# Sorted block attention and a gated feed-forward block on one core: half of batch 0's q goes as fp32 through SP's queue, turns use the full array height, later heads' matrices are built later

## The chip, the core and the metric

The kernel runs on one core of one Trainium2 chip. The metric is the device time of one execution in microseconds (us). A core has TensorE (PE, matrix products, with its weight loads shown apart as PEld), VectorE (DVE), ScalarE (ACT), GpSimd (POOL) and SyncE (SP). All of them work at the same time, each through its own instructions in order, and wait for each other by semaphores. DMA transfers are issued here by POOL and by SP; each of the two has a queue of its own, and 16 DMA engines serve both. Inputs lie in HBM, working tiles in SBUF, and PE writes its results to the eight banks of PSUM, from which ACT or VectorE evict them.

## The reference

Batch 4, 8 heads, 768 positions, head width 64; 8 blocks of 96 positions. A small matrix per head is normalised five times over rows and columns (Sinkhorn). It then mixes the blocks of k and v, each block of q attends to its mixed block of k and v, and the result goes through a gated feed-forward block.

```python
P = sort_net                                   # (4, 8, 8, 8)
for _ in range(5):
    P = P - np.max(P, axis=-1, keepdims=True)
    P = np.exp(P)
    P = P / (np.sum(P, axis=-1, keepdims=True) + 1e-09)
    P = P / (np.sum(P, axis=-2, keepdims=True) + 1e-09)
k_sorted = np.einsum('bhij,bhjcd->bhicd', P, k_b)      # v_sorted likewise
scores = scale * np.matmul(q_b, k_sb.transpose(0, 1, 2, 4, 3))
scores = scores - np.max(scores, axis=-1, keepdims=True)
attn = np.exp(scores)
attn = attn / (np.sum(attn, axis=-1, keepdims=True) + 1e-09)
x = np.matmul(attn, v_sb)                      # heads side by side: (3072, 512)
g = x @ w_gate                                 # (3072, 1536)
out = (g * (1.0 / (1.0 + np.exp(-g))) * (x @ w_val)) @ w_out
```

## The kernel before

**Tiling.** The 3072 rows are cut into eight units `u` of 384 rows, two halves (four blocks of 96) of each batch. For each unit the attention of four pairs of heads `hp` is computed, its result is laid into a transposed tile `xt`, and the feed-forward block runs over 12 chunks `m` of its 1536 columns: `g` and `u` are the two up projections (L520), `th`, `gs`, `us`, `h` and `hp` the gate around them, `dn` and `oc` the down projection and the output (L548, L554). Everything is computed in bf16 with sums in fp32; the Sinkhorn steps are in fp32.

**Order.** The program is a flat list of steps. After the loads and the five Sinkhorn iterations, which are ordinary Python code, the string `ORDER` names every step with its arguments, the engine of its eviction (`a` for ACT, `d` for VectorE) and its PSUM banks (`p0` to `p7`). Each step issues its instructions on each engine's queue at that place, so the string fixes the order of work on every engine, and of the loads that POOL issues (`ldk`, `ldv`, `ldq`, `ldwg`, `ldwv`, `ldwo`).

**Loads.** All large inputs are fp32 in HBM and become bf16 on the way into SBUF; POOL issues these transfers. The order on POOL's queue is: q of batch 0, first half (`load_q0(0)`, L199), k and v of batch 0 (L189, L193), then the identity matrix is made, then the first third of the two up weights (L208), then q's second half. In the Sinkhorn loop's first iteration POOL makes some constants (`selk`, `selm`, `rmb`); behind them it issues v, weights and k of batch 1. SP issues only the small `p_sb` load at the start, and much later the outputs and a round trip of v through HBM. POOL waits before an issue until the transfer that POOL issued eight before it has landed (seen in the profile's waits).

**Start.** The Sinkhorn loop (L330 to L367) alternates one exponential on ACT (L331) with six small operations on VectorE (L332 to L337). Meanwhile PE runs filler products (`busy`, L245, whose results nobody reads) and turns q's first half: `q0_piece(half, n, eng, b)` (L249) turns four heads, one 64-wide head at a time into the upper or lower half of the partitions (L257, 12 products for one piece), and evicts the bank into `q0t`. Piece 0 is issued in iteration 3, piece 1 in iteration 4; behind piece 1 PE has fillers and four products that read `q0t` (L346). After the loop `make_zk` spreads the normalised matrices over partitions (L376 on PE, L380 and L381 on VectorE), and `make_bdk` makes the matrix `bdk` (L384) that mixes the blocks of one batch: batch 0's at once on VectorE, the others in the step `late` (L390), whose three `make_bdk` run on POOL.

**First unit.** `kp,0,n,eng,bank` mixes and turns the piece `n` of six of batch 0's k (L283, evicted into `kt` at L238 by ACT or L240 by VectorE); `v0f,n` does the same with v, and `v0t` turns it back (L302). `tqk` makes the scores of a pair of heads (L404) and needs all six pieces of `kt`; `tmax` takes their maxima on VectorE (L420), `tmt` turns these on PE (L424), `tst` makes the scores again with the maxima subtracted (L433), `texp` is the exponential on ACT (L440), `tav` the product with v (L447), `tdiv` the division on VectorE (L453, L455), `txt` the turn into `xt` (L460). `q0p,1,n` is `q0_piece` for the second half of batch 0's q. Later batches mix v with L309 (`vp`), and the units from 2 on use `qk`, `rmax`, `shift`, `expo`, `rsum`, `norm`, `turn` and `av`.

Of the kernel before, what the change touches and what calls it, by code (L numbers as in the profile page):

```python
# [9 lines left out]
FP32 = mybir.dt.float32  # L10
BF16 = mybir.dt.bfloat16
# [4 lines left out]


ORDER = """
ldwv,2 ldwg,2 late,p0 kp,0,5,a,p1 ldwo,2 kp,0,3,d,p2 kp,0,4,a,p3 ldq,1 kp,0,2,d,p4 kp,0,0,d,p5 v0f,3,a,p6
v0f,2,a,p7 v0f,5,a,p0 kp,0,1,d,p1 tqk,0,1,p2,p3 tmax,0,1 tqk,0,2,p4,p5 tqk,0,3,p6,p7 tmax,0,3 busy,3,p0 tmt,0,1,a  # L20
busy,1,p0 tst,0,1 tmax,0,2 tmt,0,3,a tqk,0,0,p0,p1 texp,0,1 busy,1,p2 tmt,0,2,a tmax,0,0 tst,0,3 texp,0,3 tst,0,2
tmt,0,0,a v0f,1,d,p2 v0f,0,a,p3 tst,0,0 texp,0,0 ldv,2 texp,0,2 ldwo,0 v0f,4,d,p6 busy,3,p2 v0t,0,0,d,p7
v0t,1,0,d,p2 v0t,0,1,a,p3 tav,0,0,p0,p1 tdiv,0,0 v0t,1,1,a,p6 tav,0,1,p4,p5 tdiv,0,1 busy,2,p2 txt,0,0,d,p7
tav,0,2,p2,p3 tdiv,0,2 tav,0,3,p0,p1 txt,0,1,d,p6 q0p,1,0,a,p4 q0p,1,1,a,p5 txt,0,2,a,p7 g,0,2,p2,0,2 g,0,1,p3,0,2
# [85 lines left out]
def kernel(  # L110
# [16 lines left out]
    nc = tc.nc  # L127

    B, H, S, D = q.shape
# [6 lines left out]
    UT = HB * BLK  # L136
# [8 lines left out]
    C0 = UT // 128  # L145

    const = ctx.enter_context(tc.tile_pool(name="const", bufs=1))
    natp = ctx.enter_context(tc.tile_pool(name="natp", bufs=1))
# [5 lines left out]
    hpool = ctx.enter_context(tc.tile_pool(name="hpool", bufs=2))  # L154
# [10 lines left out]
    def ps(name, shape, dt=FP32, parts=128):  # L165
        n = 1
        for x in shape:
            n *= x
        t = banks[:, int(name[1:]), :]
        t = (t if dt is FP32 else t.bitcast(BF16))[0:parts, 0:n]  # L170
        if len(shape) == 1:
            return t
        if len(shape) == 2:
            return t.rearrange("p (a b) -> p a b", a=shape[0])
        return t.rearrange("p (a b c) -> p a b c", a=shape[0], b=shape[1])
# [6 lines left out]
    kn, qn, vn = {}, {}, {}  # L182
# [4 lines left out]
    def load_k(b):  # L187
        kn[b] = natp.tile([128, CK, D], BF16, name="kn", tag="kv", bufs=4)
        nc.gpsimd.dma_start(out=kn[b], in_=k[b].rearrange("h (j ch c) d -> (h j ch) c d", j=NB, ch=CH))  # L189

    def load_v(b):
        vn[b] = natp.tile([128, CK, D], BF16, name="vn", tag="kv", bufs=4)
        nc.gpsimd.dma_start(out=vn[b], in_=v[b].rearrange("h (j ch c) d -> (h j ch) c d", j=NB, ch=CH))  # L193

    def load_q0(half):
        if half == 0:
            qh = natp.tile([128, 2, H, C0, D], BF16, name="qh", tag="qn", bufs=2)
            qn[0, 0], qn[0, 1] = qh[:, 0], qh[:, 1]
        nc.gpsimd.dma_start(out=qn[0, half],  # L199
                            in_=q[0][:, ds(half * UT, UT), :].rearrange("h (p c) d -> p h c d", c=C0))  # L200

    def load_q(b):
        qn[b] = natp.tile([128, H, S // 128, D], BF16, name="qn", tag="qn", bufs=2)
# [2 lines left out]
    def load_w(dst, w, n):  # L206
        f = ds(n * (DF // 3), DF // 3)
        nc.gpsimd.dma_start(out=dst[:, :, f], in_=w.rearrange("(hp p) f -> p hp f", p=128)[:, :, f])  # L208

    def load_ws(n):  # L210
        load_w(wg_sb, moe_w_gate, n)
        load_w(wv_sb, moe_w_val, n)
# [5 lines left out]
    p_sb = const.tile([BH, NB + 1, NB], FP32, name="p_sb")  # L218
    nc.sync.dma_start(out=p_sb[:, 0:NB, :], in_=sort_net.rearrange("b h i j -> (b h) i j"))
    load_q0(0)  # L220
    load_k(0)
    load_v(0)
    ident = const.tile([128, 128], BF16, name="ident")
    make_identity(nc, ident)
    load_ws(0)
    load_q0(1)

    fill = const.tile([128, 512], BF16, name="fill")
# [7 lines left out]
    def evict(eng, dst, src):  # L236
        if eng == "a":
            nc.scalar.copy(dst, src)  # L238
        else:
            nc.vector.tensor_copy(dst, src)  # L240

    def busy(n, b, cols=512):

        for _ in range(n):
            nc.tensor.matmul(ps(b, [cols]), lhsT=fill[:, 0:128], rhs=fill[:, 0:cols], start=True, stop=True)  # L245
# [3 lines left out]
    def q0_piece(half, n, eng, b):  # L249
        if ("q", half) not in tr:  # L250
            q0t = trp.tile([128, 2, HP, HB, BLK], BF16, name="q0t", tag="qt")
            tr["q", 0], tr["q", 1] = q0t[:, 0], q0t[:, 1]
        p = ps(b, [6, 128], BF16)
        for l in range(6):
            hp, c = 2 * n + l // C0, l % C0
            for x in range(2):
                nc.tensor.transpose(p[ds(64 * x, 64), l, :], qn[0, half][:, 2 * hp + x, c, :], ident)  # L257
        dst = tr["q", half][:, ts(n, 2)].rearrange("p hp i (cq c) -> p hp (i cq) c", c=C0)
        evict(eng, dst, p.rearrange("p (hp c) n -> p hp n c", c=C0))

# [69 lines left out]
    for it in range(N_ITER):  # L330
        nc.scalar.activation(P, P, AF.Exp)  # L331
        nc.vector.reduce_sum(rowred[:, :, 0], P, axis=AX.X)  # L332
        nc.vector.reciprocal(rowred, rowred)
        nc.vector.tensor_mul(P, P, rowred.to_broadcast([BH, NB, NB]))
        nc.vector.reduce_sum(colred[:, 0, :], p_sb.transpose([0, 2, 1]), axis=AX.X)
        nc.vector.reciprocal(colred, colred)
        nc.vector.tensor_mul(pbf if it == N_ITER - 1 else P, P,  # L337
                             colred.to_broadcast([BH, NB, NB]))
        if it == N_ITER - 2:
            q0_piece(0, 0, "a", "p0")  # L340
        if it == N_ITER - 1:
            q0_piece(0, 1, "a", "p1")
            busy(8, "p7", 112)
            busy(10, "p7")
            for _ in range(4):
                nc.tensor.matmul(ps("p7", [UT]), lhsT=fill[:, 0:128], rhs=tr["q", 0][:, HP - 1].rearrange("p i c -> p (i c)"),  # L346
                                 start=True, stop=True)
        if it == 0:
            selk = const.tile([BH, BH, 16], BF16, name="selk")
            nc.gpsimd.tensor_copy(selk, ident[0:BH, 0:BH].unsqueeze(2).to_broadcast([BH, BH, 16]))  # L350
            nc.gpsimd.memset(v0[:, :, :, :, D:D + 1], 1.0)

            sel = const.tile([128, HB], BF16, name="sel")
            nc.gpsimd.tensor_tensor(sel, ident[:, 0:HB], ident[:, 64:64 + HB], op=ALU.add)
            selm = const.tile([128, HB, BLK], BF16, name="selm")
            nc.gpsimd.tensor_scalar(selm, sel.unsqueeze(2).to_broadcast([128, HB, BLK]), -1.0, None, op0=ALU.mult)

            rmb = [const.tile([BLK, 2, 64], BF16, name=f"rmb{n}") for n in range(HP)]
            for t in rmb:
                nc.gpsimd.memset(t, 0.0)  # L360
        if it == 1:
            mjk = const.tile([128, 1, NB], FP32, name="mjk")
            nc.vector.reduce_sum(mjk[:, 0, :], ident.rearrange("p (h j ch) -> p j h ch", j=NB, ch=CH),
                                 axis=AX.XY)
        if it == 2:
            m1 = const.tile([128, 8, CH], FP32, name="m1")
            nc.vector.reduce_sum(m1, ident.rearrange("p (h j ch) -> p h ch j", j=NB, ch=CH), axis=AX.X)  # L367
# [4 lines left out]
    def make_zk(b0, b1, b):  # L372
        n = (b1 - b0) * NB
        p = ps(b, [n, NB])
        for b in range(b0, b1):
            nc.tensor.matmul(p[:, ts(b - b0, NB)].rearrange("p i j -> p (i j)"),  # L376
                             lhsT=selk[:, ds(b * H, H), :].rearrange("p h r -> p (h r)"),
                             rhs=pbf.rearrange("p i j -> p (i j)"), start=True, stop=True)
        zk = const.tile([128, n, NB], FP32, name=f"zk{b0}")
        nc.vector.tensor_tensor(zk, p, mjk.to_broadcast([128, n, NB]), op=ALU.mult)  # L380
        nc.vector.reduce_sum(zkr[:, b0:b1, :].rearrange("p b i -> p (b i)"), zk, axis=AX.X)  # L381

    def make_bdk(b, eng):
        eng.tensor_tensor(  # L384
            bdk[:, b],
            m1.unsqueeze(2).to_broadcast([128, H, NB, CH]),
            zkr[:, b, :].unsqueeze(1).unsqueeze(3).to_broadcast([128, H, NB, CH]),
            op=ALU.mult)

    def late(b):  # L390
        make_zk(1, B, b)
        for n in range(1, B):
            make_bdk(n, nc.gpsimd)

# [159 lines left out]
    def ffn_last(u, t, n, eng, b):  # L556
# [19 lines left out]
        busy=busy, late=late, ldk=load_k, ldv=load_v, ldq=load_q, ldwo=load_wo,  # L576
        ldwg=lambda n: load_w(wg_sb, moe_w_gate, n), ldwv=lambda n: load_w(wv_sb, moe_w_val, n),
        q0p=q0_piece, v0f=v0_piece, v0t=v0_turn, kp=k_piece, vp=v_piece, qp=q_piece, vtrip=v_turn,
        tqk=t_qk, tmax=t_max, tmt=t_maxt, tst=t_st, texp=t_exp, tav=t_av, tdiv=t_div, txt=t_xt,
        qk=qk, rmax=rowmax, shift=shift, expo=expo, rsum=rowsum, norm=norm, turn=turn, av=av,  # L580
        g=lambda *a: ffn_up(wg_sb, "g", *a), u=lambda *a: ffn_up(wv_sb, "u", *a), th=ffn_th, us=ffn_us, gs=ffn_gs,
        h=lambda u, m: ffn_h(u, m, False), hp=lambda u, m: ffn_h(u, m, True), dn=ffn_down, oc=ffn_out, dl=ffn_last)
# [33 lines left out]
```

## Time and profile before

| what | us |
|---|---|
| median of 3 runs (265.08 to 265.35) | 265.09 |
| the profiled execution: its time | 265.16 |
| the profiled execution: its span on the core | 263.1 |
| first scores (L404) start | 17.14 |
| first feed-forward product (L520) starts | 30.16 |
| PE busy with L520, weights wg and wv | 79.8 and 79.6 |
| PE busy with L548 | 70.5 |

The span runs from the core's first to its last instruction; the time of a run has some 2 us more around it. The busy time of PE counts the length of every product, and neighbours overlap, so a busy share of 97% says that PE almost always had something in work.

The transfers of the first 40 us, each with the moment of its issue on POOL, the time from issue to landing, and the first instruction that reads it:

| transfer | issued | to landing | first read |
|---|---|---|---|
| q of batch 0, half 0 | 1.24 | 5.6 | 6.84 (L257) |
| k of batch 0 | 2.31 | 8.1 | 13.00 (L283) |
| v of batch 0 | 2.86 | 12.2 | 15.08 (L283) |
| first third of w_gate | 3.95 | 13.7 | 30.16 (L520) |
| first third of w_val | 4.71 | 15.5 | 32.39 (L520) |
| q of batch 0, half 1 | 5.45 | 16.7 | 29.19 (L257) |
| v of batch 1 | 9.13 | 16.7 | 31.84 (L309) |
| k of batch 1 | 11.26 | 23.3 | 38.42 (L283) |

In the profile, PE, PEld, DVE, ACT and POOL are the engines, L283 is line 283 of the kernel, and `out<-in` names the tiles that an instruction writes and reads. A bracket at a row's end gives the idle time of the engine ahead of the instruction and what ended it. `x48` counts instructions merged into one row.

### The profile page before, as it was taken

The page shows a single profiled execution, that of the slowest core. Times are in us where ns is not written, and L with a number is a line of the kernel's source. Part 1 is how long each engine was busy: PE and PEld are TensorE (multiplying, and loading weights), DVE is VectorE, ACT ScalarE, POOL GpSimd, SP SyncE. Part 2 cuts the span into 40 slices and gives each one's busy share as a digit, 9 for nine tenths or more (in the row PEclk, how much of TensorE's full clock was granted, in tenths as well). Part 3 has the DMA queues.
Part 4 walks back from the last instruction along what each step waited for, and adds up shares of the span by engine and source line. Part 5 has one row for each costly group of instructions (what it writes and reads, how often), then busy time and mean ns, then how long its engine had stood idle before and what let it go on. Part 6 is the DMA issues. An engine that isn't in the chain of part 4 may idle for free.

```text
span 263.1 us, 6835 instructions
## 1 busy us (share of the span) xinstructions
PE 254.7 (97%) x2766; PEld 157.1 (60%) x2766; DVE 190.3 (72%) x345; ACT 154.2 (59%) x299; POOL 116.8 (44%) x152
## 2 busy tenths in 40 slices
PE   7878999999999999999999999999999999999995
PEld 7456766665566555665566555665566555655553
DVE  5775877689688896779798776977897778632460
ACT  3246787755467467866476767586566665544422
POOL 8732342433856437135632475226544672431220
PEclk9999999999999999999999999999999999999999
DMA  6999999999980902100294005920110021002103
GB/s 82 215 199 209 216 203 211 204 238 248 157 195 0 161 2 82 44 0 2 120 118 123 2 0 199 118 49 1 52 70 0 2 80 42 0 1 83 40 0 120
DMA packets 33695, 25.60 MB, mean 97 GB/s; under 512 B 21376, under 2 KB 29312, under 8 KB 33664
## 3 DMA queue, kind: packets, MB, share of 16 engines
q0 software_dynamic: 11104, 14.16, 31.4%
q1 hardware_dynamic: 22560, 11.02, 18.2%
q8 instruction: 21, 0.34, 0.5%
q14 instruction: 10, 0.08, 0.1%
HBM read 30.68 MB, written 8.65 MB: 149 GB/s over the span
## 4 chain that ended last, share of the span: by engine, by line
PE 88%; DMA 5%; DVE 3%; issue 1%; ACT 1%; POOL 1%; DVEq 0%; POOLq 0%
PE ps_ps L520 47%; PE ps_ps L548 23%; DMA vn<-in_v_dram 5%; PE ps_ps L497 3%; PE ps_ps L404 3%; PE ps_ps L283 3%; PE ps_ps L508 2%; PE ps_ps L309 2%; PE ps_ps L433 1%; PE ps_ps L270 1%; PE ps_ps L560 1%; DVE qt L240 1%; DVE xn L455 1%; PE ps_ps L447 1%; DVE v L240 0%
## 5 line engine op out<-in xcount | busy, mean ns | idle before, releaser
L539 POOL TENSOR_TENSOR h<-u_sb,gs 128x384 bf16<-128x384 f32 x65 | 58.6, 911 | 64.9 <-DVE gs L533 36.3
L520 PE MATMUL ps_ps<-xt,wg_sb 128*128 128x384 bf16 x384 | 79.8, 327 | 0.0
L520 PE MATMUL ps_ps<-xt,wv_sb 128*128 128x384 bf16 x384 | 79.6, 326 | 0.0
L533 DVE SCALAR_TENSOR_TENSOR gs<-th,ps_ps 128x384 bf16<-128x384 bf16 x96 | 51.4, 543 | 32.4 <-ACT th L525 32.0
L548 PE MATMUL ps_ps<-wo_sb,h 128*128 128x512 bf16 x276 | 70.5, 380 | 0.0
L525 ACT ACTIVATE th<-ps_ps 128x384 bf16<-128x384 f32 x96 | 46.9, 490 | 34.2 <-PE ps_ps L520 32.1
L490 POOL TENSOR_TENSOR en<-e,rs 96x384 bf16<-96x384 f32 x48 | 38.5, 822 | 55.6 <-DVE rs L485 31.1
L520 PEld LDWEIGHTS <-wv_sb 128*128 128x128 bf16 x384 | 37.2, 98 | 24.8
L520 PEld LDWEIGHTS <-wg_sb 128*128 128x128 bf16 x384 | 35.5, 98 | 25.9
L548 PEld LDWEIGHTS <-h 128*128 128x128 bf16 x276 | 26.3, 98 | 25.3 <-issue 0.2
L529 ACT ACTIVATE u_sb<-ps_ps 128x384 f32<-128x384 f32 x65 | 31.8, 490 | 10.9 <-PE ps_ps L520 7.6
L480 ACT ACTIVATE e<-e 96x768 f32<-96x768 f32 x24 | 20.2, 841 | 23.8 <-DVE e L477 23.8
L484 DVE TENSOR_REDUCE rs<-e 96x8 f32<-96x768 f32 x24 | 22.6, 941 | 10.3 <-ACT e L480 10.3
L473 DVE TENSOR_REDUCE rm<-ps_ps 96x8 f32<-96x768 f32 x24 | 22.8, 949 | 4.8 <-PE ps_ps L404 4.3
L477 DVE TENSOR_TENSOR e<-ps_ps,rm 96x768 f32<-96x768 f32 x24 | 22.9, 953 | 0.8
L541 DVE SCALAR_TENSOR_TENSOR h<-ps_ps,gs 128x384 bf16<-128x384 f32 x31 | 17.2, 557 | 2.7
L238 ACT COPY o_sb<-ps_ps 128x512 f32<-128x512 f32 x16 | 9.2, 580 | 8.6 <-PE ps_ps L548 8.6
L497 PEld LDWEIGHTS <-en 96*96 96x96 bf16 x192 | 12.0, 125 | 3.2
L245 PE MATMUL ps_ps<-fill 128*128 128x112 bf16 (+1 forms) x96 | 11.7, 290 | 2.2 <-DVE p_sb L322 1.5
L497 PE MATMUL ps_ps<-ident,en 96*96 96x96 bf16 x192 | 12.5, 209 | 0.0
L238 ACT COPY et<-ps_ps 96x768 bf16<-96x768 bf16 x13 | 10.3, 791 | 3.2 <-PE ps_ps L497 3.1
L238 ACT CAST kt<-ps_ps 128x512 bf16<-128x512 f32 x14 | 7.8, 593 | 3.8 <-PE ps_ps L283 3.7
(97 smaller groups left out, 240.6 us busy)
## 6 DMA issues: line engine op xcount, KB each, us to landing
out_dram<-o_sb SPq DMA_DIRECT2D x23, 256.0 KB, 2.0
kn<-in_k_dram POOLq DMA_DIRECT2D x4, 768.0 KB, 18.6
vn<-in_v_dram POOLq DMA_DIRECT2D x4, 768.0 KB, 14.4
qn<-in_q_dram POOLq DMA_DIRECT2D x3, 768.0 KB, 23.6
vscr<-vm SPq DMA_DIRECT2D x3, 768.0 KB, 3.3
vt<-vscr SPq DMA_DIRECT2D x3, 768.0 KB, 7.9
wg_sb<-in_moe_w_gate_dram POOLq DMA_DIRECT2D x3, 512.0 KB, 18.7
wv_sb<-in_moe_w_val_dram POOLq DMA_DIRECT2D x3, 512.0 KB, 20.4
```

Of the source, the lines that this page charges most:

```text
L238: nc.scalar.copy(dst, src)
L473: nc.vector.reduce_max(m[:, :, :, 0], st["s", u, hp], axis=AX.X)
L477: nc.vector.tensor_tensor(e, st["s", u, hp], st["m", u, hp].to_broadcast([BLK, 2, HB, BLK]), op=ALU.subtract)
L484: nc.vector.reduce_sum(rs[:, :, :, 0], st["e", u, hp], axis=AX.X)
L490: nc.gpsimd.tensor_tensor(en[:, x], st["e", u, hp][:, x], st["rs", u, hp][:, x].to_broadcast([BLK, HB, BLK]), op=ALU.mult)
L497: nc.tensor.transpose(p[:, x * HB + i, :], st["en", u, hp][:, x, i, :], ident[0:BLK, 0:BLK])
L520: nc.tensor.matmul(st[kind, u, m], lhsT=w[:, kc, ts(m, 128)], rhs=xt[u][:, kc, :], start=(kc == 0), stop=(kc == HP - 1))
L525: nc.scalar.activation(st["th", u, m], st["g", u, m], AF.Tanh, scale=0.5)
L529: nc.scalar.activation(st["us", u, m], st["u", u, m], AF.Copy, scale=0.5)
L533: nc.vector.scalar_tensor_tensor(gs, st["th", u, m], 1.0, st["g", u, m], op0=ALU.add, op1=ALU.mult)
L539: nc.gpsimd.tensor_tensor(h_t[u][:, m, :], st["us", u, m], st["gs", u, m], op=ALU.mult)
L548: nc.tensor.matmul(st["o", u, t], lhsT=h_t[u][:, m, ts(t, 128)], rhs=wo_sb[:, m, :], start=(m == 0), stop=(m == NFC - 1))
```

## The change

Four things change.

1. The first half of batch 0's q goes as fp32 into a tile of the pool of `h`, by two transfers of four heads each that SP issues right after `p_sb`. A new step `cast_q0` casts it to bf16 and lays the heads side by side: four heads on ACT after Sinkhorn iteration 1, the other four on POOL after iteration 2. The second half still comes by POOL's queue as bf16, now into a tile of that same pool, and POOL lays its heads side by side by two `cast_q0` in `late`.
2. With two heads side by side, `q0_piece` turns both by one product of the full width: 6 products for a piece instead of 12.
3. POOL makes the identity matrix before it issues the loads of k and v. The fillers around the two pieces of q are distributed anew.
4. In `ORDER`, `late` (with `make_zk` for batches 1 to 3, their `make_bdk`, and the two casts) moves from near the front, where it stood behind two weight loads, to the place after the last maximum of the first unit, behind the issue of two more loads. The last piece of k (`kp,0,1`) moves from behind the three first pieces of v to before them; the banks shift accordingly, and one filler ahead of `tmt,0,2` becomes two.

```diff
-ldwv,2 ldwg,2 late,p0 kp,0,5,a,p1 ldwo,2 kp,0,3,d,p2 kp,0,4,a,p3 ldq,1 kp,0,2,d,p4 kp,0,0,d,p5 v0f,3,a,p6
-v0f,2,a,p7 v0f,5,a,p0 kp,0,1,d,p1 tqk,0,1,p2,p3 tmax,0,1 tqk,0,2,p4,p5 tqk,0,3,p6,p7 tmax,0,3 busy,3,p0 tmt,0,1,a
-busy,1,p0 tst,0,1 tmax,0,2 tmt,0,3,a tqk,0,0,p0,p1 texp,0,1 busy,1,p2 tmt,0,2,a tmax,0,0 tst,0,3 texp,0,3 tst,0,2
+ldwv,2 ldwg,2 kp,0,5,a,p1 ldwo,2 kp,0,3,d,p2 kp,0,4,a,p3 ldq,1 kp,0,2,d,p4 kp,0,0,d,p5 kp,0,1,d,p6 v0f,3,a,p7
+v0f,2,a,p0 v0f,5,a,p1 tqk,0,1,p2,p3 tmax,0,1 tqk,0,2,p4,p5 tqk,0,3,p6,p7 tmax,0,3 busy,3,p0 tmt,0,1,a
+busy,1,p0 tst,0,1 tmax,0,2 tmt,0,3,a tqk,0,0,p0,p1 texp,0,1 busy,2,p2 tmt,0,2,a tmax,0,0 late,p2 tst,0,3 texp,0,3 tst,0,2
...
     def load_q0(half):
+        src = q[0][:, ds(half * UT, UT), :].rearrange("h (p c) d -> p h c d", c=C0)
+
         if half == 0:
-            qh = natp.tile([128, 2, H, C0, D], BF16, name="qh", tag="qn", bufs=2)
+            qh = natp.tile([128, 2, C0, H, D], BF16, name="qh", tag="qn", bufs=2)
             qn[0, 0], qn[0, 1] = qh[:, 0], qh[:, 1]
-        nc.gpsimd.dma_start(out=qn[0, half],
-                            in_=q[0][:, ds(half * UT, UT), :].rearrange("h (p c) d -> p h c d", c=C0))
+
+            qn["f", 0] = hpool.tile([128, H, C0, D], FP32, name="qf", tag="h")
+            for n in range(2):
+                h = ds(n * (H // 2), H // 2)
+                nc.sync.dma_start(out=qn["f", 0][:, h], in_=src[:, h])
+        else:
+            qn["f", 1] = hpool.tile([128, H, C0, D], BF16, name="qg", tag="h")
+            nc.gpsimd.dma_start(out=qn["f", 1], in_=src)
+
+    def cast_q0(half, n, act):
+        h = ds(n * (H // 2), H // 2)
+        (nc.scalar.copy if act else nc.gpsimd.tensor_copy)(qn[0, half][:, :, h, :].transpose([0, 2, 1, 3]),
+                                                           qn["f", half][:, h])
...
     load_q0(0)
+    ident = const.tile([128, 128], BF16, name="ident")
+    make_identity(nc, ident)
     load_k(0)
     load_v(0)
-    ident = const.tile([128, 128], BF16, name="ident")
-    make_identity(nc, ident)
     load_ws(0)
     load_q0(1)
...
             hp, c = 2 * n + l // C0, l % C0
-            for x in range(2):
-                nc.tensor.transpose(p[ds(64 * x, 64), l, :], qn[0, half][:, 2 * hp + x, c, :], ident)
+            nc.tensor.transpose(p[:, l, :], qn[0, half][:, c, ds(2 * hp, 2), :].rearrange("p x d -> p (x d)"), ident)
...
+        if it == 1:
+            cast_q0(0, 0, True)
+        if it == 2:
+            cast_q0(0, 1, False)
         if it == N_ITER - 2:
             q0_piece(0, 0, "a", "p0")
+            busy(20, "p7", 112)
+            busy(4, "p7")
         if it == N_ITER - 1:
             q0_piece(0, 1, "a", "p1")
-            busy(8, "p7", 112)
-            busy(10, "p7")
+            busy(5, "p7")
...
         for n in range(1, B):
             make_bdk(n, nc.gpsimd)
+        for n in range(2):
+            cast_q0(1, n, False)
```

## The prediction

> **What bounds the kernel now.** I read the page first: busy times, then the chain that ended last.
>
> ```profile
> span 263.1 us, 6835 instructions
> PE 254.7 (97%) x2766; PEld 157.1 (60%) x2766; DVE 190.3 (72%) x345; ACT 154.2 (59%) x299; POOL 116.8 (44%) x152
> PE 88%; DMA 5%; DVE 3%; issue 1%; ACT 1%; POOL 1%; DVEq 0%; POOLq 0%
> ```
>
> PE makes 88% of the chain. The timeline of PE shows it without a gap from 31 us to the end (one of 0.29 us at 59.4), so nearly whatever the first 31 us give or lose reaches the end one to one. The one DMA of the chain is v of batch 0. Then the chain in order of time, cut to the first scores (start, length, what):
>
> ```profile
> 2.86 12.18 DMA vn<-in_v_dram
> 15.04 0.04 issue
> 15.08 0.97 PE ps_ps L283 x48
> 16.05 1.09 ACT vT L238 x2
> 17.14 0.01 issue
> 17.14 0.74 PE ps_ps L404 x24
> ```
>
> v lands at 15.04, PE mixes three pieces of it, and the first scores (L404) begin at 17.14. The view names ACT's vT as the last step, but the scores read kt. So I looked at VectorE (start, length, engine, line, operation):
>
> ```profile
> 12.46 0.29 DVE L384 TENSOR_TENSOR bdk<-m,zkr 128x128 bf16<-128x128 f32 x1
> 13.11 0.36 DVE L380 TENSOR_TENSOR zk<-ps_ps,mjk 128x192 f32<-128x192 f32 x1 [0.36 <-PE ps_ps L376]
> 13.50 0.35 DVE L381 TENSOR_REDUCE zkr<-zk 128x24 f32<-128x192 f32 x1
> 13.77 1.88 DVE L240 CAST kt<-ps_ps 128x512 bf16<-128x512 f32 x3
> 16.40 0.69 DVE L240 CAST kt<-ps_ps 128x512 bf16<-128x512 f32 x1 [0.76 <-PE ps_ps L283]
> 17.66 0.95 DVE L420 TENSOR_REDUCE rmb<-ps_ps 96x8 bf16<-96x768 f32 x1 [0.57 <-PE ps_ps L404]
> ```
>
> The last kt piece ends at 17.09, and the scores follow 0.05 later. It is late because its matmuls (piece 1) stand behind the three v pieces on PE, hence behind v's landing.
>
> **Part 1: piece 1 of k ahead of v, and zk of the later heads out of the way.** PE's rows at this place:
>
> ```profile
> 12.81 0.26 PE L376 MATMUL ps_ps<-pbf,selk 32*128 32x64 bf16 x3
> 13.00 1.46 PE L283 MATMUL ps_ps<-bdk,kn 128*64 128x64 bf16 x80
> 15.08 0.95 PE L283 MATMUL ps_ps<-bdk,vn 128*64 128x64 bf16 x48 [0.63 <-DMA vn<-in_v_dram]
> ```
>
> Without L376 x3 the k pieces start at 12.81 instead of 13.00, one each 0.29 (1.46 for five), six end at 14.55. VectorE's first kt needs the second piece: before 13.00 + 2x0.29 + 0.19 (from matmuls to eviction, as ACT's first kt: 13.29 to 13.48) = 13.77; now 13.58. The four of VectorE run at steps of 0.60 ((1.88-0.69)/2), the last ending at 13.58 + 3x0.60 + 0.69 = 16.07. Scores at 16.1 instead of 17.14: **-1.04**. Condition: PE's three v pieces (0.95) are done by then, so v lands by 15.1. ACT's three evictions of v (1.56) end near 16.6; ACT is next wanted at 18.93-1.04.
>
> **Part 2: does v land by 15.1?** Before, the first packets of q ran at 3.0, and v landed 12.04 later. Now q half 0 is issued by SP's queue right after p_sb, whose issue took 0.39 from 0.74 and whose packets began at 1.6; so q's begin near 2.0, the two issues taking 0.33 each on a queue with nothing else until 53.9. The transfer writes 786 KB instead of 393. From 7 to 10 us POOL's queue wrote 213 GB/s of bf16, read from twice as many fp32 bytes, 427; SP's queue moved 418 in and out at 130 us. So I count the larger side, 786 KB either way, 1.9 us, and v lands near 2.0 + 12.0 = 14.0 to 14.5. If written bytes counted (213), 1.85 more: about 16.1; the 418 speaks against it. k lands at 10.4 now and has until 12.8.
>
> **Part 3: the casts.** ACT's stands between the exponentials of iterations 1 and 2. The first ends at 4.86, the second starts at 6.37. 128x768 cost ACT 0.77 (q0t), 96x768 fp32 0.84: I take 0.8. It costs nothing if q's first half is there by 5.55. Packets of 768 B came at 98 in the first us, then 139, 215 and 253 per half us; 512 of them from 2.0 need 2.25, and the semaphore some 0.5 (q landed at 6.84): 4.8. If SP's queue starts at full rate, 3.8. Cover 0.7 us; beyond it every exponential and the bdk behind them move one to one.
> POOL's cast: q's issue (1.07) leaves POOL's start, so the work that ends at 9.13 ends at 8.06. POOL's COPY took 642 ns for 512 elements a partition, for 768 that is 0.96; by the rate of its two-input h (911 for 384), 1.82. A copy is the nearest row: it ends at 9.0 (9.9). PE turns (0.5), ACT evicts (0.77), four L346 (0.82) and then zk at 11.73: due at 9.6. Zero, at worst +0.3. POOL's next loads, issued from 9.13, start from 9.0. The identity (0.24 and 0.29) now precedes k's issue, which still comes at about 1.8 instead of 2.31. The fp32 tile and the bf16 one of half 1 use the two buffers of h; h is first written after 30 us: no wait.
>
> **Part 4: full turns.** The 24 half turns of a half batch take 0.86: 0.22 plus 23 steps of 28 ns, since two run side by side. Eight full-height turns of vT (L302) took 0.63, or 57 ns a step. Twelve full ones: 0.22 + 11x0.057 = 0.85. **0.** The bound below is 28 ns a step, -0.33. Dearer ones (a weight load of 98 each, +0.3) would be covered: VectorE works nearly without gap from 26.85 to 31.0 and sets the end there.
>
> **Part 5: what comes back later.** `late` and one more filler now stand between the first maxima and the second scores:
>
> ```profile
> 20.96 0.38 PE L245 MATMUL ps_ps<-fill 128*128 128x512 bf16 x1 [0.72 <-ACT ett L440]
> 21.17 0.21 PE L424 MATMUL ps_ps<-ident,rmb 96*128 96x96 bf16 x1
> ```
>
> From 20.96 to 23.9 PE has no gap and ends in the last v piece, which VectorE awaits at 24.01. One more filler takes 0.21 (20.96 to 21.17), three L376 take 0.19 (12.81 to 13.00): **+0.40**. If something beside PE had slack there, 0. VectorE's zk and reduction (0.71) fit its 1.60 idle before 22.89. POOL's three bdk (1.13) and two casts of half 1 (0.96 each) now stand behind the issue of the next q, 22.47+0.88, and end at 26.4, at the dear rate 28.1; the turns want them at 28.6, bdk's reader L309 at 31.2. Behind them waits the load of the next v (26.39): no change. The later loads have slack: k of batch 1 lands at 34.56 and is read at 38.42, the tightest.
>
> **Sum**: -1.04 + 0.40 = -0.64. Span 262.5; the profiled run took 265.16, 2.06 around its span and 0.07 above the median. Against the median: **264.45**, said as 264.5.
>
> **Rivals.**
> (a) *Late fp32 q, slower.* k's transfer starts near 3.3 and shares the engines with q. If q's first half lands after 5.55, ACT holds the exponential; from 6.2 the gain is eaten. At 6.84, where q lands now, +1.3: 265.7. How the queues share is shown only later, with SP's 128 B packets against POOL's 6 KB ones:
>
> ```profile
> q1 hardware_dynamic: 561, 0.07, 97.6%
> q0 software_dynamic: 8, 0.05, 59.3%
> ```
>
> 70 to one, in q's favour. Against that, around 57.8 SP's 6 KB packets went 28 to 33, near one to one. At one to one for 768 B, some 23 packets on each engine would wait 0.45 each for a k packet, 10 us; but q's size is nearer the 128 B row. [...]
> (b) *Part 5 is hidden, or full turns are cheaper*: 264.05, down to 263.7. For: PE waited 0.72 just before. Against: no idle of PE afterwards.
> (c) *v late*, because written bytes count: v at 16.1, scores at 17.15, so only part 5 remains: 265.5.
> (d) *POOL's cast dear*: +0.3, 264.8.
>
> **Chances.** Forecast 0.42, (a) 0.26, (b) 0.16, (c) 0.10, (d) 0.06. No change means within 0.2%, 0.53 us (264.56 to 265.62), about what a measurement can tell. The forecast lies only 0.1 below this edge; I give 0.32 of its 0.42 to faster, 0.10 to the same. Faster: 0.32 + 0.16 = 0.48. Slower: (a) 0.24 and 0.04 of (c), 0.28. Same: 0.24. The range 263.8 to 265.9 takes in (c), (d), most of (b) and (a) up to a half that lands near 7; the forecast's own is 264.1 to 264.8.
>
> **What the next profile would show.** Right: q's first half before 5.55, exponential 2 still at 6.37, bdk at 12.46, kt's last eviction at 16.1 with the first scores behind it, v landed before 15.1, two fillers and L376 x3 near 20. Wrong: an ACT exponential waiting on the q load or its cast; PE's L376 later than 11.73; first scores released by v; PE idle on a DMA after 31 us.

## The result and the profile after

The changed kernel takes 272.12 us (median of 4 runs, 271.84 to 272.87) against 265.08 before: 1.0272 times as long, 95% interval 1.026 to 1.0284. The forecast was 264.5 with a range up to 265.9; the kernel is 7 us slower, and the range missed it by far. The page after, in the same rows as before (span, busy time of PE, the clock that PE was granted in 40 slices, the chain by engine and by line):

```profile
span 270.0 us, 6817 instructions
PE 256.4 (95%) x2754; PEld 158.4 (59%) x2754; DVE 190.7 (71%) x345; ACT 155.0 (57%) x300; POOL 118.2 (44%) x154
PEclk9869999999999999999999999999999999999999
PE 88%; DMA 5%; DVE 4%; issue 1%; ACT 1%; POOL 0%; SPq 0%; DVEq 0%
PE ps_ps L539 46%; PE ps_ps L567 22%; DMA qf<-in_q_dram 5%; PE ps_ps L516 3%; PE ps_ps L423 3%; PE ps_ps L295 2%; PE ps_ps L527 2%; PE ps_ps L258 2%; PE ps_ps L321 1%; PE ps_ps L452 1%; PE ps_ps L282 1%; DVE kt L253 1%; PE ps_ps L579 1%; DVE qt L253 1%; DVE xn L474 1%
```

The one transfer on the chain was v; now it is `qf`, the fp32 q. And the clock row, 9 in every slice before, falls to 8 and 6 in slices 2 and 3. The chain in order of time (start, length, what):

```profile
1.64 12.49 DMA qf<-in_q_dram
14.13 0.05 issue
14.18 0.83 POOL qh L212
15.02 0.05 issue
15.06 0.82 PE ps_ps L269 x6
15.88 2.13 PE ps_ps L258 x5
18.02 1.13 PE ps_ps L363 x4
19.14 0.13 PE ps_ps L393
...
20.91 2.49 DVE kt L253 x4
23.40 0.04 issue
23.45 0.74 PE ps_ps L423 x24
```

SP issued q's second half at 1.64; it landed at 14.13. POOL's cast waited for it, PE's second piece of q (L269) for the cast, and behind it in PE's order stood the fillers, the four products on `q0t` (L363) and zk (L393), at 19.08 instead of 11.73. The rows of these waits in the changed kernel:

```profile
14.18 0.82 POOL L212 CAST qh<-qf 128x768 bf16<-128x768 f32 x1 [6.29 <-DMA qf<-in_q_dram]
15.06 0.82 PE L269 MATMUL ps_ps<-ident,qh 128*128 128x128 bf16 x6 [6.35 <-POOL qh L212]
19.08 0.20 PE L393 MATMUL ps_ps<-pbf,selk 32*128 32x64 bf16 x1
```

And zk's product in the kernel before:

```profile
11.73 0.18 PE L376 MATMUL ps_ps<-pbf,selk 32*128 32x64 bf16 x1
```

The first half, issued at 1.18, had landed 3.4 us after its issue, and ACT cast it from 4.76.

Split at these marks, the spans account for the whole difference. (1) zk starts 7.35 later; from its start to the end of bdk it takes 1.02 before, 1.03 after. (2) From the end of bdk to the first scores it was 4.39 us and is 3.34: -1.05. (3) From the first scores to the first L309 (now L321) it was 14.70 and is 14.86: +0.16. (4) From there to the issue of the last output 228.65 in both, and from that issue to the span's end 2.61 before, 3.04 after: +0.43. Together 6.9, and the spans are 263.1 and 270.0. The rest of the kernel is only shifted.

### The profile page after: what moved, and what is told of

It is laid out like the page before. It is cut to its first block, busy times and chain, and to the rows that moved or that the text cites. A ratio compares the mean times of both kernels' runs of the same rounds, so it can differ in the third digit from the quotient of the medians.

```text
span 270.0 us, 6817 instructions
## 1 busy us (share of the span) xinstructions
PE 256.4 (95%) x2754; PEld 158.4 (59%) x2754; DVE 190.7 (71%) x345; ACT 155.0 (57%) x300; POOL 118.2 (44%) x154
## 4 chain that ended last, share of the span: by engine, by line
PE 88%; DMA 5%; DVE 4%; issue 1%; ACT 1%; POOL 0%; SPq 0%; DVEq 0%
PE ps_ps L539 46%; PE ps_ps L567 22%; DMA qf<-in_q_dram 5%; PE ps_ps L516 3%; PE ps_ps L423 3%; PE ps_ps L295 2%; PE ps_ps L527 2%; PE ps_ps L258 2%; PE ps_ps L321 1%; PE ps_ps L452 1%; PE ps_ps L282 1%; DVE kt L253 1%; PE ps_ps L579 1%; DVE qt L253 1%; DVE xn L474 1%
## 5 line engine op out<-in xcount | busy, mean ns | idle before, releaser
L548 ACT ACTIVATE u_sb<-ps_ps 128x384 f32<-128x384 f32 x65 | 31.8, 490 | 10.9 <-PE ps_ps L539 7.6
L258 PE MATMUL ps_ps<-fill 128*128 128x112 bf16 (+1 forms) x108 | 13.7, 294 | 2.2 <-DVE p_sb L334 1.5
```

Of the source, the lines that this page charges most:

```text
L548: nc.scalar.activation(st["us", u, m], st["u", u, m], AF.Copy, scale=0.5)
```

## The experiments

**What the two queues did while q was late.** In the changed kernel's trace, the queues from 6 to 12 us (packets, MB, share of the 16 engines; q0 is POOL's queue, q1 is SP's):

```profile
q0 software_dynamic: 201, 1.14, 91.5%
q1 hardware_dynamic: 206, 0.16, 10.4%
```

One packet of q, 768 B, went for each packet of k and v, 6 KB. Until k's first packets, q had the engines to itself (445 packets from 3 to 4 us); from 5 us on it got 31 or 32 a us (48 in one) until k and v were nearly through at 12. That gave the theory: the two queues take turns packet by packet, and the late half then holds POOL and PE, which work in order. The rivals: fp32 is simply too many bytes; or other parts of the change carry a part of the loss.

**The order alone.** The kernel before, with only the three lines of `ORDER` of the diff.

> The kernel before with the new step order alone: piece 1 of k ahead of v, late behind the last maximum, two fillers; q as before by POOL's queue. Theory (all of the loss hangs on the second half of the fp32 q): the order alone keeps the gain that the changed kernel's trace still shows inside its delay, 1.05 us from bdk to the first scores less 0.16 to 0.40 behind them, so 264.2 to 264.5 us. Rival (the moved zk and fillers take it all back, or later loads do): 265.1 or more.

Measured: 264.33 us (11 runs) against 265.03 for the kernel before, ratio 0.9975, interval 0.9966 to 0.9984. (The ratios below are to the kernel before, too.) So the order, `late`, and the filler together are a gain of 0.70, and the whole loss belongs to the other three parts of the change. PE around v and the first scores:

```profile
12.92 1.71 PE L283 MATMUL ps_ps<-bdk,kn 128*64 128x64 bf16 x96
15.23 0.95 PE L283 MATMUL ps_ps<-bdk,vn 128*64 128x64 bf16 x48 [0.59 <-DMA vn<-in_v_dram]
16.20 0.74 PE L404 MATMUL ps_ps<-kt,q0t 64*96 64x96 bf16 x24
```

All six k pieces now run in one stretch ahead of v, which still lands at 15.2. The scores start at 16.20; VectorE's last eviction of kt ends at 16.14 (13.66 + 2.48).

**k and v later.** POOL makes its constants before it issues k and v of batch 0.

```diff
     make_identity(nc, ident)
+    v0 = trp.tile([BLK, 2, HP * HB, 2, D + 2], BF16, name="v0", tag="vt")
+    selk = const.tile([BH, BH, 16], BF16, name="selk")
+    nc.gpsimd.tensor_copy(selk, ident[0:BH, 0:BH].unsqueeze(2).to_broadcast([BH, BH, 16]))
...
+    for t in rmb:
+        nc.gpsimd.memset(t, 0.0)
     load_k(0)
     load_v(0)
...
-        if it == 0:
-            selk = const.tile([BH, BH, 16], BF16, name="selk")
...
```

> The changed kernel, but POOL makes its constants (2.9 us) before it issues k and v of batch 0, so that these start when q is nearly through. Theory (q's packets of 768 B take turns one to one with k's and v's of 6 KB): q's second half lands near 5.3 instead of 14.1, POOL's cast ends before 9.6, zk is back near 11.8, and the time is 264.2 to 265 us; v must land by 15.1. Rival (fp32 q is simply too many bytes for the engines): q lands early but v lands as much later, near 16 or more, and the time stays above 267.

Measured: 265.16 us (265.07 to 265.85), ratio 1.001, interval 1.0001 to 1.0019: 7 us of the loss are gone, with the same bytes. q's second half landed 4.5 us after its issue (at 6.2), 7.9 sooner than in the changed kernel, and v only 1.9 later (4.87 + 10.9 = 15.8). So it is not the number of bytes. v missed the 15.1 that was asked for, though, and PE mixes it from 15.81 without a wait only because zk is late too, at 13.10. This profile is of the slowest of the 11 runs, 265.85; zk is 1.3 later in it than in the order alone, and the reason is a new one. POOL, then VectorE:

```profile
7.76 0.87 POOL L212 CAST qh<-qf 128x768 bf16<-128x768 f32 x1
```

```profile
7.67 0.19 DVE L357 RECIPROCAL rowred<-rowred 32x8 f32<-32x8 f32 x1
7.90 0.82 DVE L358 TENSOR_TENSOR p_sb<-p_sb,rowred 32x64 f32<-32x64 f32 x1
8.75 0.27 DVE L359 TENSOR_REDUCE colred<-p_sb 32x8 f32<-32x72 f32 x1
```

A product of the Sinkhorn loop that takes 0.21 everywhere in the trace before lasts 0.82, to just behind the end of POOL's cast. The product of the iteration before, at 6.31, lasted 0.80 while POOL issued loads; why is not shown, for the one at 5.54 met such an issue too and kept 0.21. Together they cost 1.2 us, on the loop that everything waits for.

**Small packets for k and v.** Both, for batch 0, in tiles whose rows break every 8 positions, so that each packet is 1 KB.

```diff
-        kn[b] = natp.tile([128, CK, D], ...)
-        nc.gpsimd.dma_start(out=kn[b], in_=k[b].rearrange("h (j ch c) d -> (h j ch) c d", j=NB, ch=CH))
+        t = natp.tile([128, CK // 8, 8 * D + 16], ...)[:, :, 0:8 * D]
+        nc.gpsimd.dma_start(out=t, in_=k[b].rearrange("h (j ch g c) d -> (h j ch) g (c d)", j=NB, ch=CH, c=8))
```

> The changed kernel, with k and v of batch 0 in tiles whose rows break every 8 positions, so that each packet is 1 KB (2 KB read) instead of 6 KB; nothing is issued sooner or later. Theory (one packet of each queue in turn): the 18 turns that q's second half still needs on each engine at 5.0 cost some 0.1 us each instead of 0.5, so it lands at 7 to 7.5, POOL's cast does not wait, zk near 11.8, time 264.2 to 265.2 us. Rival (bandwidth by bytes, or the queues' priority): landing stays near 14, time near 272.

Measured: 265.69 us (8 runs): three at 264.70 to 264.88, five at 265.66 to 265.84. q's second half landed 4.2 us after its issue, POOL's cast ran at 8.44 without a wait, zk at 11.95. The loss is gone, but the run does not show that the packets' size did it: POOL took 1.02 us to issue this k instead of 0.74, k's packets began a us later (one before 5 us, against 25), and by then q had little left to send.

**Smaller packets for q.** This run decides between turns by packet and grouped packets.

```diff
-            qn["f", 0] = hpool.tile([128, H, C0, D], FP32, name="qf", tag="h")
+            qn["f", 0] = hpool.tile([128, H, C0, D + 2], FP32, name="qf", tag="h")[:, :, :, 0:D]
...
-                nc.sync.dma_start(out=qn["f", 0][:, h], in_=src[:, h])
+                for c in range(C0):
+                    nc.sync.dma_start(out=qn["f", 0][:, h, c], in_=src[:, h, c])
```

> The changed kernel, but the fp32 q tile has 66 floats a row and SP issues it in six transfers, so that q comes in packets of 256 B, three times as many, each half the size of a row group no longer. Theory (one packet of each queue in turn, whatever its size): each engine must move 192 packets; some 50 are through when k starts at 4.0, then one goes per 6 KB packet of k and v (0.5 us each) until about 12, then about 12 a us beside the weights; the first half lands near 14 and holds the exponential on ACT, the second near 20; time above 278. Rival (small packets of equal power of two are grouped, as 70 of 128 B to one in the trace before): both halves land by 7, time 264.5 to 266.

Measured: 279.17 us (one run), as the turns said. The queues from 5 to 10 us:

```profile
q0 software_dynamic: 179, 1.00, 97.8%
q1 hardware_dynamic: 169, 0.04, 6.3%
```

179 packets of 6 KB, 169 of 256 B: 25 times the bytes for POOL's queue, and yet one for one; the rival's grouping does not show. ACT's cast of the first half ran at 17.80 instead of the 14 expected, POOL's at 23.2 instead of 20; between, the six issues themselves were held on SP (one for 7.29 us), which turns of packets alone do not give. From 12 to 18 us, when the weights' packets of 1 KB ran, it was 934 of them to 937 of 256 B: one for one again.

**PE kept warm.**

```diff
+            busy(29, "p7")
             q0_piece(0, 1, "a", "p1")
```

> The changed kernel with 29 more fillers of 512 columns on PE ahead of the second piece of q, which fill the 6.35 us in which PE waits for POOL's cast. Theory (the idle PE loses its clock, 0.57 granted from 15 to 19.5 us, and that alone adds some 2.1 us to the chain: 1.3 in five fillers, 0.5 in L363, 0.3 in the turns): zk near 17.0 instead of 19.1, time 270.0 us. Rival (only the landing counts): 272.1, unchanged.

Measured: 270.69 us (270.44 and 270.94), 1.4 less than the changed kernel, where 2.1 were expected; zk at 17.29, 1.79 earlier, of which 0.24 was lost again between the first scores and L321. The stretches of PE in the changed kernel (stretch, length, busy, clock granted, DMA share, GB/s):

```profile
core 0: us, PE busy (x), PEclk, DMA share, GB/s
5.00:10.00 5.00, 3.71 (x58) 1.00 1.03 219
10.00:15.00 5.00, 0.00 (x0) 0.70 1.11 211
15.00:19.50 4.50, 4.44 (x18) 0.57 1.37 200
```

and in this one, with fillers in the gap:

```profile
10.00:15.00 5.00, 5.00 (x24) 1.00 1.12 211
15.00:17.40 2.40, 2.39 (x17) 1.00 1.24 206
```

So of the 7.35 us, about 1.8 were the clock that PE lost while it stood still: five fillers took 2.34 instead of 1.24, L363 1.33 instead of 0.81. In the changed kernel PE stood still from 8.71 to 15.06, and the granted clock was 1.00 until 12 and 0.50 from 13 to 18; with the fillers in the gap it was 1.00 from 5 to 17.4.

**The waiter moved.** POOL's cast behind the issue of k of batch 1, the piece of q behind the first scores; 13 fillers ahead of zk take the place of the five and of the four products on `q0t`.

```diff
-        if it == 2:
-            cast_q0(0, 1, False)
...
-            q0_piece(0, 1, "a", "p1")
-            busy(5, "p7")
...
+            busy(13, "p7")
...
     load_k(1)
+    cast_q0(0, 1, False)
...
-tqk,0,1,p2,p3 tmax,0,1 tqk,0,2,p4,p5
+tqk,0,1,p2,p3 tmax,0,1 q0p,0,1,a,p1 tqk,0,2,p4,p5
```

> The changed kernel with POOL's cast behind the issue of k of batch 1, and the second piece of q turned behind the first scores instead of ahead of zk; 13 fillers keep PE busy until zk. q's second half still lands near 14. Theory (the loss is not the landing but what stands behind it in order on POOL and PE): zk at 11.8, first scores at 16.1, the later scores wait some 0.7 us for the piece: 264.9 to 265.6. Rival (a q that lands at 14 costs some 7 us wherever it is waited for): above 270.

Measured: 266.9 us (266.48 and 267.32), 1.3 above the upper end of what was expected and 5 below the changed kernel. q lands as late as before (POOL casts it at 14.28), and zk is at 12.09, the first scores at 16.45: so 5 of the 7 us hung on the order behind the wait. The miss: in the profile, of the slower run (267.32), PE waited 0.89 for the piece, and it was granted a clock of 0.76 from 17 to 20 us and 0.67 from 20 to 23; three fillers at 18.70 took 1.46 instead of 0.82. What lowered the clock is not shown: no wait of PE from 12 us up to there is longer than 0.9 us. How much of the miss was the clock in the other run (266.48) is not shown either.

**The second cast on ACT.** The kernel with small packets of k and v, with one word changed.

```diff
-            cast_q0(0, 1, False)
+            cast_q0(0, 1, True)
```

> The kernel with small packets of k and v, whose runs fell into two groups (264.7 to 264.9 and 265.7 to 265.8), with the second cast on ACT instead of POOL. Theory (a two-input operation of VectorE that meets POOL's cast lasts until the cast ends: 0.40 in that kernel, 0.82 in the one with k later, instead of 0.21): no such operation behind 7.5 us any more, one group near 264.7. Rival (the groups come from the landing of q or from elsewhere): two groups again.

Measured: 264.56 us, 11 runs within 264.46 to 264.66, ratio 0.9979, interval 0.9968 to 0.9991. One group, and no stretched product behind 7.5 us. In the profile of the kernel with POOL's cast, one such product at 8.94 lasted 0.40, begun inside the cast (8.44 to 9.25); that the runs of its slower group met a longer one is only inferred, since the profile fell on a run of the faster group.

This run also answers the rival that other parts of the change carry a part of the loss. With q in time (and k and v in small packets), the fp32 q, both casts, the full turns and the new fillers together are 0.23 above the order alone, and the last output is even issued 0.13 sooner (259.62 against 259.75); what is left of the 7 us is the longer end, below.

**Part 5 of the prediction: one filler less, and `late` once more.** Two steps on the order alone.

```diff
-texp,0,1 busy,2,p2 tmt,0,2,a
+texp,0,1 busy,1,p2 tmt,0,2,a
```

> The order alone (264.33) with one filler instead of two ahead of tmt,0,2. Theory (part 5: the second filler stands on the path): 264.1, 0.2 less. Rival (it lies beside other work): 264.3, unchanged.

Measured: 264.11 us (264.0 to 264.3), ratio 0.9964, interval 0.9951 to 0.9976: 0.22 less, as said. This is the fastest version of the study. Then `late`:

```diff
-tmax,0,0 late,p2 tst,0,3
+tmax,0,0 tst,0,3
...
-v0f,4,d,p6 busy,3,p2 v0t,0,0,d,p7
+v0f,4,d,p6 late,p2 busy,2,p2 v0t,0,0,d,p7
```

> The order with one filler (264.11), with late moved once more, behind the last piece of v, where PE waits for VectorE's eviction and runs three fillers (two now). Theory (the three zk matmuls are the rest of part 5, 0.19 on the path): 263.9. Rival (VectorE's zk and reduction, 0.71, then stand in the way of the v evictions): 264.1 or more.

Measured: 264.61 us, 0.5 more instead of 0.2 less. PE at that place:

```profile
22.73 0.26 PE L376 MATMUL ps_ps<-pbf,selk 32*128 32x64 bf16 x3
23.92 0.38 PE L245 MATMUL ps_ps<-fill 128*128 128x512 bf16 x1 [0.93 <-DVE zk L380]
24.35 1.50 PE L302 MATMUL ps_ps<-ident,vT 128*96 128x128 bf16 x24
```

The filler writes bank `p2`, in which zk stands until VectorE has read it, and VectorE first evicts the v piece. So PE waits 0.93, and the turns of v (L302) start at 24.35 instead of 23.89 in the run before. This was a mistake in the choice of the bank, and says nothing of `late` at that place with a bank of its own.

**The last 0.4 us.**

```diff
     nc.sync.dma_start(out=p_sb[:, 0:NB, :], in_=sort_net.rearrange("b h i j -> (b h) i j"))
+    for n in range(2):
+        extra = const.tile([BH, NB, NB], FP32, name=f"extra{n}")
+        nc.sync.dma_start(out=extra, in_=sort_net.rearrange("b h i j -> (b h) i j"))
```

> The order alone (264.33), with two more 8 KB transfers on SP's queue at the start that nobody reads. All kernels with the fp32 q so far end 3.0 to 3.1 us after the issue of the last output, those without it 2.6 to 2.7. Theory (two more transfers on SP's queue lengthen the program's end): 3.0 to 3.1 here too, time 264.5 to 264.7. Rival (the longer end belongs to the fp32 tile or the casts): 2.65, time 264.3.

Measured: 264.60 us, ratio 0.9986, interval 0.9977 to 0.9996, 0.27 above the order alone. The issue of the last output, in the order alone and here:

```profile
259.75 0.33 SPq L564 DMA_DIRECT2D out_dram<-o_half  x1
```

```profile
259.56 0.33 SPq L567 DMA_DIRECT2D out_dram<-o_half  x1
```

It is 0.19 sooner here, and the span still ends at 262.6 instead of 262.4: 3.04 us behind that issue instead of 2.65. So two more transfers of 8 KB on SP's queue cost 0.4 of span at the end. What the program does there is not shown.

## Why the prediction was wrong

**Part 3 failed, in its POOL half.** It said that POOL's cast "ends at 9.0 (9.9)", "Zero, at worst +0.3". That term was worked out from POOL's own work alone: when POOL would come to the cast, and how long the cast takes. When q's second half would be there was worked out nowhere; the sum had a landing for the first half only, 4.8 (its 2.25 for 512 packets is 2.12 by its own rows), and took the second for granted. The first half did land in time (4.6, cast at 4.76) and POOL's cast did take 0.82, but it began at 14.18, behind a landing at 14.13, and the term was +7.35.

**Rival (a) had the mechanism and the wrong victim.** It named the place (an engine in order behind a late q, for it ACT and the first half), the row (28 to 33 packets around 57.8, near one to one) and the price ("some 23 packets on each engine would wait 0.45 each"), and then set it aside because the row with 70 to one was nearer in size. Size was the wrong measure: packets of 768 B and of 256 B both went one to one here (206 to 201, 169 to 179). The price was right: from 5 to 12 us 237 of q's packets went, 15 on each engine, so one in 0.47 us. Why the 128 B packets of vt went 70 to one (561 to 8) is open.

**Part 2 was right for the wrong reason.** v landed at 13.9 (2.15 + 11.7), the forecast 14.0 to 14.5. But the forecast had all of q ahead of k and v, and about half of its 1024 packets were still unsent when k's began at 4 us. Where nearly all of q did go first (k and v later, issued 2.7 us later there), v landed at 15.8, past the 15.1 that Part 2 had to keep.

**Part 1 was right.** -1.04 was forecast; the changed kernel shows -1.05 from bdk to the first scores, inside the delay. The order alone measures -0.70 against a sum of -0.64.

**Part 4 was right.** Twelve full turns of q's half 1 took 0.83 in the changed kernel, 24 half turns 0.86 before.

**Part 5 was too dear in the changed kernel, and its filler exact.** +0.40 was forecast, +0.16 found in the changed kernel and +0.20 in the order alone. The filler, measured alone, costs 0.22 against the 0.21 forecast; so the three zk products, forecast at 0.19, cost close to nothing: with one filler, first scores to L309 take 14.65, and 14.70 before.

**Not in the sum at all**: the clock that PE lost in its wait of 6.35 us (granted 0.50 from 13 to 18 us; 1.8 of the 7.35), VectorE's products that took longer beside POOL's work (0.42 at 5.35 and 0.37 at 6.34 instead of 0.21, which put the exponential of iteration 2 at 6.74 instead of 6.37 and is hidden here behind the wait for q), and the longer end (0.43).

## What to carry to other kernels

Give every transfer that something waits for a landing of its own in the sum, each half if it is issued in halves; the time at which an engine comes to its work is only one of two terms. When a transfer moves to a second queue, count packets, not bytes: packets of 256 and 768 B got one turn here for each big one of the other queue (169 to 179 and 206 to 201; those of 128 B went 561 to 8, and why is open). So let such a transfer finish before the big ones start, or leave it where it was. And what stands in order behind a waiting instruction can cost more than the data: here moving the waiter took back 5 of 7 us, with q as late as ever.

## What the runs showed of the hardware that was not expected

- Two queues on the same 16 engines: 206 packets of 768 B to 201 of 6 KB, 169 of 256 B to 179 of 6 KB, and 937 of 256 B to 934 of 1 KB. Cutting q's packets to a third made it later, 279.17 us against 272.12. The rows of 128 B packets in the kernel before, 561 to 8 from 71.4 to 72.2 us, are the exception.
- A product of VectorE with two inputs (0.21) lasted 0.82 and 0.40 beside POOL's cast and up to 0.80 beside its other work, while reductions and reciprocals kept their 0.19 to 0.27. Beside the cast it ended 0.09 behind the cast's own end both times (8.72 and 8.63, 9.34 and 9.25). Not each such product beside POOL's work was stretched: in the kernel before, the one at 7.91 kept 0.21 beside POOL's `selm` (7.41 to 8.59). Why it did, and the others did not, is not shown.
- Two 8 KB transfers more on SP's queue at the start lengthened the span's end by 0.4 us, from 2.65 to 3.04 behind the last issue.
